# The second network's first loads join a fixed instruction order, and w_v's rebuilding stands behind it

## The chip, the cores and the metric

The kernel runs on one core of a Trainium2 chip. The metric is the device time of one execution in microseconds. A core has a matrix engine (PE), a vector engine (DVE), a scalar engine (ACT), a general engine (POOL) and an engine that issues transfers (SP). Each takes its own instructions in the order in which they stand, and waits on semaphores for the others.

## What is computed

Causal attention with a decay over 32 heads (4 batches of 8 heads, 576 positions, 64 features), then two feed-forward networks. Cut to what matters:

```
attn = softmax(q k^T / 8 + cum_i - cum_j, causal);  x = attn @ v          # 4 x 576 x 512
h = relu(x @ w_in); u, v = split(h)                                       # network 1
x = (u * (w_spatial @ layernorm(v) + b_spatial)) @ w_out
xk = mu_k * x + (1 - mu_k) * x_prev;  xr = mu_r * x + (1 - mu_r) * x_prev # network 2
out = sigmoid(xr @ w_r) * (relu(xk @ w_k)^2 @ w_v)
```

The weights come as 64-bit numbers.

## The kernel before, in words

*Work and names.* Attention goes by pairs of heads. `s` and `t` are scores and transposed scores (matmuls of `kT`, `qT` and the helper rows `kA`, `qA`), `nm` and `mrow` their row maxima, which go through a DRAM buffer `md` into `qA`, and `e` the exponentials; pv multiplies `e` by `v` into `o`. Between them PE does network 1 for the batches that are ready: m1v and m1u are the two halves of x @ w_in (`xt` by `win`), evacuated by ACT into `v` and `u`; `mv` is the normalization of `v`, `vn` its result; m2 (`m<-wspT,vn` in the profile) multiplies by w_spatial, and DVE multiplies its result into `u` (`u<-m,sw,u`). The products go to DRAM as `gd`.

*The second part.* It goes by five chunks of 512 positions. m3(i) loads a chunk as four `g` from `gd`, and splits each into a high and a low part (`gh`): ACT casts, DVE subtracts. It then multiplies by w_out in 48 matmuls. `mix` makes `xx`; m4, m5 and m6 multiply by w_k, w_v and w_r. A weight is rebuilt in blocks of 128x512 by `weights2`: a load into one of two staging buffers `wst`, one ACT and three DVE instructions into `we`, and a split by ACT and DVE into the weight (`moe_w_v` and so on in the profile). Some blocks are rebuilt early, during attention (`emoe_w_k`).

*What sets the order.* Every operation up to the end of network 1 is recorded (class `Planned`) and issued by a list of numbers, `ORDER`, written out by hand; each is held in that place on its engine (`keep_in_program_order`). What comes after `k.nc.issue()` is traced directly, and a scheduler may place it between or ahead of the fixed ones. In the kernel before, m3(0) and w_v's rebuilding are such free work. w_k's and w_r's rebuilding is recorded. `SLOTS` says which buffer each recorded tile takes. The helper through which recorded and pinned operations are issued has line 291, direct ones have line 305 (292 and 306 after the change).

Of the kernel before, what the change touches and what calls it, by code (L numbers as in the profile page):

```python
# [212 lines left out]
]  # L213

# [933 lines left out]
def body(tc, a, out):  # L1148
    k = K(tc, a, out)
# [26 lines left out]
    last = G + 1.45  # L1176
# [20 lines left out]
    for _ in k.m3(0):  # L1197
        next(w2, 0)
# [61 lines left out]
```

## Time and profile before

| | us |
|---|---|
| median of 3 runs (lowest, highest) | 704.87 (704.25, 706.37) |
| the profiled execution | 705.93 |
| its span in the trace | 703.9 |
| PE busy in it | 649.9 (92%) |
| DVE, ACT, POOL busy | 418.8, 373.0, 136.9 |

The span is the time from the first to the last instruction; a little lies around it. All further times are counted from the span's start. PE's work comes to 92% of the span, so what matters is where PE stands idle and what it then waits for. From about 412 us on PE does only the second part.

### The profile page before, as it was taken

The page shows a single profiled execution, that of the slowest core. Times are in us where ns is not written, and L with a number is a line of the kernel's source. Part 1 is how long each engine was busy: PE and PEld are TensorE (multiplying, and loading weights), DVE is VectorE, ACT ScalarE, POOL GpSimd, SP SyncE. Part 2 cuts the span into 40 slices and gives each one's busy share as a digit, 9 for nine tenths or more (in the row PEclk, how much of TensorE's full clock was granted, in tenths as well). Part 3 has the DMA queues.
Part 4 walks back from the last instruction along what each step waited for, and adds up shares of the span by engine and source line. Part 5 has one row for each costly group of instructions (what it writes and reads, how often), then busy time and mean ns, then how long its engine had stood idle before and what let it go on. Part 6 is the DMA issues. An engine that isn't in the chain of part 4 may idle for free.

```text
span 703.9 us, 11693 instructions
## 1 busy us (share of the span) xinstructions
PE 649.9 (92%) x4238; PEld 463.2 (66%) x4238; DVE 418.8 (59%) x1077; ACT 373.0 (53%) x765; POOL 136.9 (19%) x343
## 2 busy tenths in 40 slices
PE   0588899999999899999998699999999999999997
PEld 0245454575655566556756587888888888888896
DVE  7788875896676766770278699355137225522341
ACT  5567875985457653565266387263246225422521
POOL 7012354254234223353322000000000000000000
PEclk9999999999999999999999899999999999999999
DMA  6976766744568437220263742201010100100010
GB/s 210 240 189 175 195 164 172 211 113 103 137 135 214 108 94 147 77 80 22 82 191 98 216 128 82 60 1 61 0 46 10 51 1 15 61 1 0 1 61 30
DMA packets 73615, 70.06 MB, mean 100 GB/s; under 512 B 50883, under 2 KB 51555, under 8 KB 73558
## 3 DMA queue, kind: packets, MB, share of 16 engines
q1 hardware_dynamic: 73126, 68.14, 36.5%
q10 hardware_dynamic: 432, 1.18, 0.5%
q8 instruction: 33, 0.54, 0.3%
q14 instruction: 24, 0.20, 0.1%
HBM read 43.78 MB, written 9.79 MB: 76 GB/s over the span
## 4 chain that ended last, share of the span: by engine, by line
PE 64%; DVE 11%; DMA 10%; ACT 5%; POOL 3%; issue 3%; SPq 3%; POOLq 0%; DVEq 0%; ACTq 0%
PE m L305 43%; PE o L291 5%; PE t L291 4%; PE s L291 3%; PE m1u L291 3%; PE m L291 3%; SPq L291 3%; DMA qA<-md 2%; PE m1v L291 2%; DVE nm L291 1%; DMA v<-in_v_dram 1%; POOL mv L291 1%; DVE junk L291 1%; ACT junka L291 1%; DMA g<-gd 1%
## 5 line engine op out<-in xcount | busy, mean ns | idle before, releaser
L305 PE MATMUL m<-xx,moe_w_k 128*128 128x512 f32 (+1 forms) x480 | 105.5, 369 | 0.0
L305 PE MATMUL m<-moe_w_v,k 128*128 128x512 f32 x432 | 104.3, 390 | 0.0
L305 PEld LDWEIGHTS m<-xx,moe_w_k 128*128 128x128 f32 x480 | 83.9, 188 | 16.2 <-ACT tmp L305 0.2
L305 PEld LDWEIGHTS m<-moe_w_v,k 128*128 128x128 f32 x432 | 80.7, 188 | 17.1
L291 ACT ACTIVATE e<-t,qa 128x512 f32<-128x512 f32 (+1 forms) x128 | 71.4, 591 | 26.8 <-PE t L291 24.0
L305 DVE TENSOR_TENSOR tmp<-tmp 128x512 f32<-128x512 f32 (+1 forms) x40 | 25.4, 638 | 92.9 <-ACT tmp L305 92.7
L291 POOL TENSOR_SCALAR_AFFINE_SELECT e<-e 128x128 f32<-128x128 f32 (+1 forms) x160 | 50.5, 330 | 130.6 <-ACT e L291 129.9
L291 PE MATMUL s<-kT,qT 128*128 128x192 f16 (+3 forms) x192 | 54.2, 291 | 13.6 <-DMA qT<-nq 7.0
L291 DVE CUSTOM_DVE_ANT_0 junk<-s,mask 128x320 bf16<-128x320 f32 (+4 forms) x100 | 47.5, 475 | 29.4 <-PE s L291 27.0
L305 ACT ACTIVATE tmp<-m 128x512 f32<-128x512 f32 (+1 forms) x40 | 22.3, 557 | 78.7 <-PE m L305 77.9
L305 PE MATMUL m<-gh,moe_w_out 128*128 128x512 f32 (+1 forms) x240 | 57.0, 386 | 5.5 <-DVE u L291 5.5
L291 PE MATMUL m1v<-win,xt 128*128 128x512 f16 x240 | 56.7, 379 | 0.0
L291 PE MATMUL m<-wspT,vn 128*128 128x288 f16 x384 | 54.2, 286 | 1.3 <-ACT u L291 1.1
L291 PE MATMUL m1u<-xt,win 128*128 128x288 f16 x384 | 52.8, 286 | 2.4 <-ACT u L291 2.3
L291 PE MATMUL t<-qA,kA 69*128 69x512 f16 (+2 forms) x192 | 48.6, 285 | 6.8 <-DMA qA<-md 5.2
L305 PEld LDWEIGHTS m<-gh,moe_w_out 128*128 128x128 f32 x240 | 44.1, 196 | 15.6 <-DVE u L291 5.8
L291 PE MATMUL s<-kA,qA 67*128 67x192 f16 (+3 forms) x192 | 49.5, 292 | 3.2 <-DMA qA<-qT 3.2
L291 PE MATMUL o<-e,v 128*64 128x64 f32 (+4 forms) x384 | 51.5, 404 | 0.3 <-ACT sm L291 0.3
L305 PE MATMUL m<-moe_w_r,xx 128*128 128x512 f32 x216 | 51.2, 394 | 0.0
L291 PE MATMUL t<-qT,kT 128*128 128x512 f16 (+2 forms) x192 | 50.1, 285 | 0.0
L305 PEld LDWEIGHTS m<-moe_w_r,xx 128*128 128x128 f32 x216 | 40.4, 187 | 9.9
L291 PEld LDWEIGHTS <-win 128*128 128x128 f16 x384 | 36.2, 98 | 13.4 <-issue 3.1
(162 smaller groups left out, 1065.1 us busy)
## 6 DMA issues: line engine op xcount, KB each, us to landing
knat<-in_k_dram SPq DMA_DIRECT2D x16, 320.0 KB
v<-in_v_dram SPq DMA_DIRECT2D x20, 256.0 KB
sr<-rd SPq DMA_DIRECT2D x32, 144.0 KB
gd<-u SPq DMA_DIRECT2D x16, 288.0 KB
out_dram<-o SPq DMA_DIRECT2D x18, 256.0 KB
qnat<-in_q_dram SPq DMA_DIRECT2D x14, 320.0 KB
wst<-in_moe_w_k_dram SPq DMA_DIRECT2D x8, 512.0 KB
g<-gd SPq DMA_DIRECT2D x16, 256.0 KB
```

The costliest lines, as they stand in the source:

```text
L291: self.tc.keep_in_program_order(fn(*map(now, a), **{x: now(y) for x, y in kw.items()}))
L305: return fn(*map(now, a), **{x: now(y) for x, y in kw.items()})
```

## The change

Three things are done. The first part of m3(0), its four loads, four casts and four subtracts, is recorded as a step `gh0` and has places in `ORDER`; the matmuls follow as before. The ACT instruction and the first DVE instruction that rebuild a block of w_v are pinned behind all that was issued before them. And `ORDER` has new numbers throughout, from the start of attention to the end of network 1 (4221 entries instead of 4209). Of the list one line is shown.

```diff
 ORDER = [
     0, 2, 9, 8, 10, 11, 1, 12, 4, 13, 14, 3, 6, 5, 7, 17, 15, 16, 29, 18, 30, 19, 20, 40,
...
-    57, 56, 36, 99, 47, 52, 54, 53, 71, 100, 101, 37, 55, 61, 72, 73, 62, 38, 233, 74, 102, 59, 103, 245,
...
+    57, 56, 71, 99, 47, 52, 54, 53, 100, 101, 36, 72, 73, 59, 55, 61, 37, 233, 102, 103, 245, 253, 74, 62,
...
     ('wstage2', 'wst'): [0, 1, 0, 1, 0, 1, 0, 1],
+    ('phase3', 'g'): [0, 1, 0, 1],
     ('wstage2', 'we'): [0, 1, 0, 1, 0, 1, 0],
...
+    def gh0(self):
+        self.m30 = self.m3(0)
+        next(self.m30)
+
...
     w2 = k.weights2(wp, ("moe_w_out", "moe2_w_k", "moe2_w_r"), wst, True)
     next(w2)
+    k.add(last + 2.6, 9, k.gh0)
     last += 1.65
...
-    w2b = k.weights2(k.p2, ("moe2_w_v",), wst)
+    w2b = k.weights2(k.p2, ("moe2_w_v",), wst, True)
     wrest = (x for w in (w2, w2b) for x in w)
-    for _ in k.m3(0):
+    for _ in k.m30:
         next(w2, 0)
```

DVE at the end of network 1, before: L305 rows are the free work, here w_v's; `u<-m_...,sw,u` is the evacuation of m2.

```order
L291 SCALAR_TENSOR_TENSOR u<-m_5014,sw,u 128x288
L291 TENSOR_TENSOR moe_w_r<-we,moe_w_r 128x512
L291 SCALAR_TENSOR_TENSOR u<-m_5032,sw,u 128x288
L305 TENSOR_SCALAR wst<-wst 128x512
L291 SCALAR_TENSOR_TENSOR u<-m_5050,sw,u 128x288
L291 TENSOR_SCALAR wst<-wst 128x512
L305 SCALAR_TENSOR_TENSOR we<-we,wst 128x512
```

The same place after the change:

```order
L292 SCALAR_TENSOR_TENSOR u<-m_5030,sw,u 128x288
L292 TENSOR_TENSOR moe_w_r<-we,moe_w_r 128x512
L292 SCALAR_TENSOR_TENSOR u<-m_5048,sw,u 128x288
L292 SCALAR_TENSOR_TENSOR u<-m_5067,sw,u 128x288
L292 TENSOR_SCALAR wst<-wst 128x512
L292 SCALAR_TENSOR_TENSOR we<-we,wst 128x512
L292 SCALAR_TENSOR_TENSOR we<-wst,we 128x512
L292 TENSOR_TENSOR moe_w_r<-we,moe_w_r 128x512
L306 SCALAR_TENSOR_TENSOR tmp<-x_5115,mu,tmp 128x511
L306 TENSOR_TENSOR xx_5162<-tmp,xx_5162 128x512
```

The first instruction on w_v stood ahead of the last `u`; after the change the last two `u` are neighbours, then come w_r's last block and the mixing, and w_v's first instruction stands 22 rows behind the last `u`.

ACT where m1v's results are evacuated, before: `gh<-g` are the casts of m3(0)'s loads.

```order
L291 CAST moe_w_k<-emoe_w_k_3799 128x512
L291 ACTIVATE v_4628<-m1v,ds 128x512
L291 CAST moe_w_k<-emoe_w_k_4008 128x512
L291 CAST moe_w_k<-emoe_w_k_4140 128x512
L305 CAST gh<-g 128x512 x2
L291 ACTIVATE v_4628<-m1v,ds 128x512
L291 ACTIVATE mv<-mv,eps 128x1
L291 ACTIVATE we<-wst 128x512
L291 ACTIVATE mv<-mv 128x1
```

The same place after the change:

```order
L292 CAST moe_w_k<-emoe_w_k_4117 128x512
L292 ACTIVATE v_4634<-m1v,ds 128x512
L292 ACTIVATE we<-wst 128x512
L292 ACTIVATE mv<-mv,eps 128x1
L292 ACTIVATE mv<-mv 128x1
L292 ACTIVATE v_4634<-m1v,ds 128x512
L292 ACTIVATE we<-wst 128x512
L292 CAST gh<-g 128x512
L292 ACTIVATE v_4634<-m1v,ds 128x512
L292 CAST vn<-v_4634 128x512
L292 ACTIVATE mv<-mv,eps 128x1
L292 CAST gh<-g 128x512
```

The two casts stood together ahead of the second `v`; now the second `v`, two `we` and two `mv` are ahead of the first cast, and the casts stand singly.

PE in the middle of attention, before, where `t` waits at 220.60 us (`m1v` is network 1, `o<-e,v` is pv):

```order
L291 LDWEIGHTS xt_209
L291 MATMUL m1v<-win,xt_209 128x512
L291 LDWEIGHTS kA_162
L291 MATMUL t<-qA_260,kA_162 128x512
L291 LDWEIGHTS kT_157
L291 MATMUL t<-qT_285,kT_157 128x512
```

The same place after the change:

```order
L292 LDWEIGHTS xt_209
L292 MATMUL m1v<-win,xt_209 128x512
L292 MATMUL o<-e,v_258 64x320 x2
L292 MATMUL o<-e,v_258 64x192 x2
L292 MATMUL o<-e,v_258 64x64 x2
L292 LDWEIGHTS kA_162
L292 MATMUL t<-qA_265,kA_162 128x512
L292 LDWEIGHTS kT_157
L292 MATMUL t<-qT_292,kT_157 128x512
```

Six matmuls of pv stand ahead of the first `t`, which had stood behind it.

## Rows read from the trace of the kernel before

**Rows 1.** The page's first line.

```profile
span 703.9 us, 11693 instructions
```

**Rows 2.** Stages: PE, PEld, DVE, ACT, POOL busy (instructions), granted clock, DMA share, GB/s.

```profile
250.00:350.00 100.00, 99.43 (x864) 64.37 (x863) 53.04 (x175) 47.40 (x102) 35.10 (x82) 1.00 0.35 88
350.00:412.00 62.00, 53.00 (x321) 37.31 (x319) 47.08 (x90) 35.08 (x70) 9.68 (x26) 0.94 0.50 151
412.00:704.00 292.00, 288.04 (x1322) 237.39 (x1320) 130.40 (x237) 119.21 (x218) 1.03 (x4) 1.00 0.10 35
```

**Rows 3.** PE's waits from 350 to 412 us: total, times, longest.

```profile
PE m L305 <- DVE u L291: 5.5, 1, 5.5
PE m1u L291 <- ACT u L291: 2.3, 1, 2.3
PE m L291 <- ACT u L291: 1.1, 1, 1.1
```

**Rows 4.** PE's timeline: start, duration, instruction, idle time before.

```profile
371.68 6.04 PE L291 MATMUL m1u<-xt,win 128*128 128x288 f16 x48 [2.33 <-ACT u L291]
378.86 1.63 PE L291 MATMUL m<-wspT,vn 128*128 128x288 f16 x12 [1.14 <-ACT u L291]
...
398.27 14.07 PE L305 MATMUL m<-gh,moe_w_out 128*128 128x512 f32 x48 [5.53 <-DVE u L291]
```

**Rows 5.** ACT's timeline from 350 us.

```profile
359.96 1.27 ACT L305 CAST gh<-g 128x512 fp32r<-128x512 f32 x2 [4.43 <-DMA g<-gd]
361.13 0.68 ACT L291 ACTIVATE v<-m1v,ds 128x512 f32<-128x512 f32 x1
...
361.90 0.65 ACT L291 ACTIVATE we<-wst 128x512 f32<-128x512 f32 x1
...
371.14 0.49 ACT L291 ACTIVATE u<-m1u,ds 128x288 f32<-128x288 f32 x1
```

**Rows 6.** DVE's timeline at the end of network 1.

```profile
394.15 0.51 DVE L291 SCALAR_TENSOR_TENSOR u<-m,sw,u 128x288 f32<-128x288 f32 x1
397.36 0.43 DVE L305 TENSOR_SCALAR wst<-wst 128x512 int32<-128x512 int32 x1 [2.70 <-DMA wst<-in_moe_w_v_dram]
397.70 0.51 DVE L291 SCALAR_TENSOR_TENSOR u<-m,sw,u 128x288 f32<-128x288 f32 x1
398.13 0.42 DVE L291 TENSOR_SCALAR wst<-wst 128x512 int32<-128x512 int32 x1
```

**Rows 7.** The chain that ended last, 374 to 400 us: start, duration, piece.

```profile
392.95 4.38 DMA wst<-in_moe_w_v_dram
```

**Rows 8.** Short windows, columns as in rows 2: the clock after waits.

```profile
398.20:404.00 5.80, 5.73 (x14) 4.48 (x15) 4.04 (x8) 1.35 (x3) 0.00 (x0) 0.50 0.58 194
...
412.00:424.00 12.00, 12.00 (x53) 9.51 (x52) 11.80 (x22) 10.26 (x19) 0.45 (x1) 1.00 0.57 178
369.00:372.00 3.00, 0.67 (x6) 0.41 (x5) 3.00 (x8) 2.14 (x6) 2.21 (x7) 1.00 0.21 72
...
110.50:113.90 3.40, 3.40 (x31) 1.69 (x30) 2.23 (x11) 0.64 (x3) 0.00 (x0) 0.50 0.60 134
```

**Rows 9.** PE's timeline in the first chunk of the second part.

```profile
431.83 2.02 PE L305 MATMUL m<-moe_w_v,k 128*128 128x512 f32 x8
...
445.68 2.91 PE L305 MATMUL m<-xx,moe_w_k 128*128 128x512 f32 x12
448.43 2.90 PE L305 MATMUL m<-moe_w_v,k 128*128 128x512 f32 x12
```

**Rows 10.** PE's waits from 40 to 350 us.

```profile
PE t L291 <- DMA qA<-md: 5.2, 5, 1.4
```

**Rows 11.** PE's timeline in attention.

```profile
110.17 0.30 PE L291 MATMUL s<-kT,qT 128*128 128x320 f16 x1 [1.63 <-DVE nm L291]
...
220.60 0.38 PE L291 MATMUL t<-qA,kA 69*128 69x512 f16 x1 [1.03 <-DMA qA<-md]
```

**Rows 12.** Waits up to 45 us.

```profile
PE s L291 <- DMA qA<-qT: 3.2, 1, 3.2
```

264 rows, old and new, of tables (ORDER, SLOTS) are left out of this document.

## The prediction

> **What bounds the kernel now.** I read the stages first. From 412 us on PE is busy in 288 of 292 us, from 250 to 350 us in 99.43 of 100; from 350 to 412 us it is busy in only 53.0 of 62 [rows 2]. So the end is set by PE's work plus PE's idle time, and the largest idle stretch after the start-up is the passage from the attention to the first weights of the second part. The list of PE's waits there has three entries, 2.3, 1.1 and 5.5 us: twice for ACT's `u`, once for DVE's `u` [rows 3]. The timeline places them: ahead of the second 48 m1u matmuls at 371.68, ahead of m2 at 378.86, and 5.53 us ahead of m3(0) at 398.27 [rows 4]. Each delays all that PE does afterwards, since PE does not wait again to speak of.
>
> Then I looked at what ACT and DVE were doing. ACT stood idle for 4.43 us and cast the first two `gh` at 359.96, when their load landed; the second `v` had to come behind them, at 361.13, and the first `u` at 371.14 [rows 5]. DVE had all but one `u` of network 1 done at 394.15; then an instruction of w_v's rebuilding, at 397.36, waited 2.70 us for its load, and the last `u` came behind it at 397.70 [rows 6]. That load was issued at 392.95 and took 4.38 us [rows 7]: three of the 5.53 us are a transfer that m3(0) has no use for.
>
> Last the clock. From 398.20 to 404 us the granted clock was 0.50, the lower of its two levels (1.2 GHz); from 412 to 424 it was 1.00, the higher (2.4 GHz) [rows 8]. The 48 matmuls of m3(0) took 14.07 us [rows 4]; at full clock 53 such matmuls take 12.00 us [rows 8], 0.226 each, and 48 take 10.9. So 3.2 us more were lost behind the gap.
>
> **The change part by part.** *(1) `gh`'s casts take places in the order.* On ACT they now stand behind two `v`, two `we` and two `mv`, and singly. A `v` with an `mv` behind it takes 361.90 - 361.13 = 0.77 us, a `we` some 0.56 (its 0.65 less the 0.1 by which such instructions overlap, as I estimate it) [rows 5]; 2 x 0.77 + 2 x 0.56 = 2.7 us. They fill 2.7 of the 4.43 us that ACT stood idle; one `gh` still holds ACT until 359.96. What follows comes 2.7 us earlier, the first `u` too. PE then finds it done at about 368.9, before its first 48 m1u matmuls end at 371.68 - 2.33 = 369.35, and the first wait vanishes. It reaches m2 2.33 us earlier, but the `u` that m2 waits for is 2.7 us earlier, so of the second wait 2.33 + 1.14 - 2.7 = 0.8 us stays, and m2 starts 2.7 us earlier. Term: 2.7 us. Bounds: 0, if another chain, that of the `mv` through DVE and POOL, sets the `u` anyway, and 3.5, both waits gone.
>
> The four loads and four subtracts that are recorded with them are the same ones as before. On SP the first two `g` stand where they stood, behind the two w_k loads; so nothing waits for them that did not before.
>
> *(2) w_v held behind the order.* The last `u` follows the one of 394.15, whose next instruction could start 0.43 us later (by the step from 397.70 to the next row, of the same kind [rows 6]), at 394.6 instead of 397.70: 3.1 us. Behind it DVE now has w_r's last block and the mixing, which m4 needs. Whether everything ahead of that `u` also comes 2.7 us earlier depends on w_r's loads, each of which waits for one of two staging buffers; these are freed by conversions that stand in the same order and come earlier too. I take the whole 2.7, so m3(0) starts 2.7 + 3.1 = 5.8 us earlier, at 392.5; the lower bound is 3.1, w_r's loads where they were.
>
> What w_v's delay costs: nothing, because PE has other work. The first m5 matmul runs at 431.83 [rows 9], and after the change at about 423. In the new order 34 DVE instructions, taken at the 0.65 us of a 128x512 `we` [rows 5], follow the last `u` up to the end of w_v's first block: 34 x 0.65 = 22 us after 392, at 414. That cover of 9 us, less what DVE waits in between, is the estimate on which the worst rival below turns.
>
> *(3) The clock.* The gap before m3(0) shrinks from 5.53 to 5.53 - 3.1 = 2.4 us. The gap of 2.33 us that ends at 371.68 left the clock at 1.00 [rows 4, 8]; against it stands 0.50 from 110.5 to 113.9 us behind a wait of 1.63 [rows 8, 11]. The gap of 2.33 is the nearer row: it followed a long run of matmuls, as the new one will. So I take full clock: 3.2 us. Bound: 0.
>
> The Trainium skill, page "TensorE: Matmul & The Clock Gate", section "Part 1: The HAM clock gate", says that idling puts the array back to half rate, that sustained activity releases it, and that the window it is watched in runs freely, so that the moment varies. The trace agrees on two levels, 1.00 and 0.50 [rows 8]. By that rule a gap of 2.4 us may or may not be punished, depending on where it falls: the sum would be 11.0 or 7.8 us. It is the first rival.
>
> *(4) The order laid out anew in attention.* PE's `t` matmuls waited for DMA qA<-md five times from 40 to 350 us, 5.2 us in all [rows 10], 1.03 of it at 220.60 [rows 11]. At three of the five places the new order puts other matmuls ahead of the waiting `t` (at 220.60 six of pv, at the two others m1u). At about 1.0 us each (5.2 / 5) that is worth up to 3; since what is put there is taken from a later place, I take half, 1.5. At the start the first `s<-kA` waited 3.2 us for qA<-qT [rows 12]; `nq` is now finished three DVE instructions earlier and its transfers go ahead of cumd. That is worth between 0 and 3.2; I take 0.5, since many other waits follow that one. Bounds for the whole: +6 (3 and 3.2) and -4: were the 100 us from 250, in which PE was idle for 0.57 [rows 2], stripped of the work that filled them, they could take on waits like the five, at most some four of 1.0.
>
> **Sum.** 2.7 + 3.1 + 3.2 + 2.0 = 11.0 us. The profiled execution took 705.93 us, 2.0 more than its span of 703.9 [rows 1]; it would take 694.9, with a span of 692.9. It was 1.06 us above the median of the runs, 704.87; from that the forecast is 693.9 us.
>
> **The rivals.** *The clock falls all the same:* all else as above, 3.2 us less: 697.1 us. For it speaks the stretch at 110 us.
>
> *w_r's loads set the last `u`:* m2 ends earlier but the last `u` stays at 394.6; then the gap is 5.53 + 2.7 - 3.1 = 5.1 us, the clock falls, and the gain is 3.1 + 2.0 = 5.1: 699.8 us. For it speaks that w_r's conversions stand between the `u` on DVE in both orders; against it, that their loads wait for conversions which move.
>
> *No change:* w_r's loads set the last `u`, and attention loses its 4 us instead of gaining 2: 3.1 - 4 = -0.9, about 705.8 us, within what can be told from no change.
>
> *Slower: w_v too late.* After w_v is held back, PE reaches an m5 before its weights are rebuilt. m4 and m5 blocks alternate at 448.43 - 445.68 = 2.75 us each [rows 9], so PE wants a block of w_v each 5.5 us. A block is a load of 4.4 us [rows 7], a DVE instruction of 0.43 [rows 6] and five more on DVE and ACT at about 0.65 (the `we` in rows 5). With two buffers these overlap and a block takes about half of their sum, 4 us; one after another they take 4.4 + 0.43 + 5 x 0.65 = 8.1, and eight blocks lose 8 x (8.1 - 5.5) = 21 us, less a cover of 5 to 9 us: 12 to 16 us, against a gain of 11. It would end at 706 to 710 us. With 5 us of cover it decides at 5.5 + (11 + 5) / 8 = 7.5 us a block. Against it: the two staging buffers are there as before, and DVE and ACT, 130 and 119 us busy of 292 [rows 2], have time to spare.
>
> *More:* attention's bound of +6 instead of 2 holds: 4 us more, 689.9, and with the second `u` wait gone too 689.1 us.
>
> **How the numbers follow.** The forecast, with a range of its own from 691 to 696, gets 0.47; the clock rival 0.19, w_r's loads 0.13; more than forecast 0.07; no change 0.07; slower 0.07. A measurement of this kernel can tell about 0.3%, 2.1 us, from no change: 702.8 to 707.0. Faster has 0.47 + 0.19 + 0.13 + 0.07 = 0.86, within 0.07, slower 0.07. The range from 688.5 to 700 leaves out no change, slower and a small part of the others.
>
> **What would show it.** Right: PE's list of waits after the attention without 2.3 and without 5.5 for DVE's `u`; the last two `u` on DVE directly one behind the other, w_v's conversion later; one `gh` alone at about 360 on ACT; granted clock 1.00 under m3(0), and its 48 matmuls in 11 us; no PE wait for moe_w_v. Wrong: m3(0) starting at 395 behind w_r, 0.50 under it, PE waits with moe_w_v in their name after 415 us, or new waits of PE between 250 and 350 us.

## The result and the profile after

The changed kernel took 696.16 us, median of 4 runs (693.02 to 698.28), beside 704.56 (702.93 to 706.37) for the kernel before: ratio 0.9864 [0.9832, 0.9896], 1.4% faster, 8.4 us. Run again in two later sets with the kernel before, it gave 0.9810 and 0.9844; the mean of the three is 0.984, 11.3 us. The forecast was 693.9, the sum 11.0 us. The profiled execution, 697.71 us, is one of the slower of its four. The page's first line after, for [rows 1]:

```profile
span 696.0 us, 11688 instructions
```

PE's list of waits after the change, from 330 to 412 us (total, times, longest), has one entry where [rows 3] had three:

```profile
PE m L306 <- DVE u L292: 2.1, 1, 2.1
```

Of its timeline (start, duration, instruction, idle time before) these rows answer to [rows 4, 9]:

```profile
351.10 13.11 PE L292 MATMUL m1v<-win,xt 128*128 128x512 f16 x60
364.05 11.92 PE L292 MATMUL m1u<-xt,win 128*128 128x288 f16 x96
375.81 1.63 PE L292 MATMUL m<-wspT,vn 128*128 128x288 f16 x12
...
391.79 13.01 PE L306 MATMUL m<-gh,moe_w_out 128*128 128x512 f32 x48 [2.10 <-DVE u L292]
404.64 4.29 PE L306 MATMUL m<-xx,moe_w_k 128*128 128x512 f32 x18
...
425.37 1.09 PE L306 MATMUL m<-moe_w_v,k 128*128 128x512 f32 x4
```

All 96 m1u run on without a wait, m2 follows at once, and m3(0) waits 2.10 us instead of 5.53. The last m1v matmuls before the passage began at 350.36 before, 0.74 us earlier than here. So attention itself came no sooner in this pair, and everything gained in it lies behind: from there to m3(0) it is 40.69 us instead of 47.91, to m4 53.54 instead of 61.82.

ACT's timeline after, for [rows 5]:

```profile
357.60 0.67 ACT L292 ACTIVATE v<-m1v,ds 128x512 f32<-128x512 f32 x1
358.64 0.70 ACT L292 ACTIVATE we<-wst 128x512 f32<-128x512 f32 x1 [0.37 <-DMA wst<-in_moe_w_k_dram]
359.29 0.62 ACT L292 CAST gh<-g 128x512 fp32r<-128x512 f32 x1
...
367.14 0.89 ACT L292 ACTIVATE u<-m1u,ds 128x288 f32<-128x288 f32 x2
```

The second `v` comes at 357.60 instead of 361.13, the first `u` at 367.14 instead of 371.14; the 4.43 us of idle time ahead of the cast are gone, and the cast no longer waits at all. Of ACT's time, 1.64 and 0.37 us now go to waits for the two w_k loads ahead of `we`. DVE's timeline after, for [rows 6], with w_v's first block:

```profile
389.43 0.51 DVE L292 SCALAR_TENSOR_TENSOR u<-m,sw,u 128x288 f32<-128x288 f32 x1
390.19 0.69 DVE L292 TENSOR_TENSOR moe_w_r<-we,moe_w_r 128x512 fp32r<-128x512 f32 x1 [0.25 <-ACT moe_w_r L292]
390.81 0.93 DVE L292 SCALAR_TENSOR_TENSOR u<-m,sw,u 128x288 f32<-128x288 f32 x2
...
416.31 0.42 DVE L306 TENSOR_SCALAR wst<-wst 128x512 int32<-128x512 int32 x1
...
420.89 0.68 DVE L306 TENSOR_TENSOR moe_w_v<-we,moe_w_v 128x512 fp32r<-128x512 f32 x1
```

The last two `u` stand together, and the first block of w_v is done at 420.89 + 0.68 = 421.6, 3.8 us before PE's first m5 at 425.37.

Windows of the trace after, columns as in [rows 2]; the second and third answer to the first of [rows 8], the last two to those of [rows 2]:

```profile
75.00:80.00 5.00, 3.92 (x30) 1.87 (x27) 4.24 (x12) 5.00 (x12) 3.82 (x8) 1.00 1.13 299
391.80:396.00 4.20, 4.20 (x11) 3.30 (x12) 2.35 (x4) 0.62 (x1) 0.00 (x0) 0.59 0.90 285
396.00:404.60 8.60, 8.60 (x38) 6.96 (x37) 3.64 (x5) 5.54 (x9) 0.00 (x0) 1.00 0.10 38
250.00:350.00 100.00, 97.58 (x847) 62.97 (x846) 54.22 (x175) 49.35 (x103) 36.76 (x85) 1.00 0.32 79
350.00:412.00 62.00, 59.90 (x360) 43.30 (x358) 48.83 (x92) 40.81 (x78) 8.86 (x27) 0.97 0.51 149
```

The clock still fell behind the gap: 0.59 granted over the first 4.2 us of m3(0), 1.00 after that. PE is now idle for 2.1 us from 350 to 412 (it was 9.0), but for 2.42 from 250 to 350 (it was 0.57).

### The profile page after: what moved, and what is told of

Read it like the earlier page. It is cut to its first block, busy times and chain, and to the rows that moved or that the text cites. A ratio compares the mean times of both kernels' runs of the same rounds, so it can differ in the third digit from the quotient of the medians.

```text
span 696.0 us, 11688 instructions
## 1 busy us (share of the span) xinstructions
PE 646.5 (93%) x4238; PEld 462.4 (66%) x4238; DVE 419.4 (60%) x1077; ACT 375.8 (54%) x765; POOL 138.7 (20%) x343
## 4 chain that ended last, share of the span: by engine, by line
PE 65%; DVE 12%; DMA 10%; ACT 5%; POOL 3%; SPq 3%; issue 3%; DVEq 0%; POOLq 0%; ACTq 0%
PE m L306 43%; PE o L292 6%; PE t L292 4%; PE s L292 4%; PE m1u L292 3%; DMA wst<-in_moe_w_k_dram 3%; DMA qA<-md 3%; SPq L292 3%; PE m L292 3%; DVE nm L292 2%; POOL mv L292 2%; DMA knat<-in_k_dram 1%; PE m1v L292 1%; DMA sr<-rd 1%; DVE junk L292 1%
## 5 line engine op out<-in xcount | busy, mean ns | idle before, releaser
L292 POOL TENSOR_SCALAR_AFFINE_SELECT e<-e 128x128 f32<-128x128 f32 (+1 forms) x160 | 53.2, 347 | 133.2 <-ACT e L292 132.3
L292 PE MATMUL s<-kT,qT 128*128 128x64 f16 (+3 forms) x192 | 54.4, 293 | 12.5 <-DVE nm L292 7.2
L292 DVE CUSTOM_DVE_ANT_0 junk<-s,mask 128x512 bf16<-128x512 f32 (+4 forms) x100 | 47.5, 475 | 23.4 <-PE s L292 20.4
L306 PE MATMUL m<-gh,moe_w_out 128*128 128x512 f32 (+1 forms) x240 | 55.5, 381 | 2.1 <-DVE u L292 2.1
L292 PE MATMUL s<-kA,qA 67*128 67x64 f16 (+4 forms) x192 | 49.8, 293 | 1.4 <-DMA kA<-cumd 1.4
L292 PEld LDWEIGHTS o<-e,v 128*64 128x64 f32 x384 | 24.7, 136 | 29.8 <-issue 18.6
```

Source lines behind the costliest of these rows:

```text
L292: self.tc.keep_in_program_order(fn(*map(now, a), **{x: now(y) for x, y in kw.items()}))
L306: return fn(*map(now, a), **{x: now(y) for x, y in kw.items()})
```

## The experiments

Every ratio is to the kernel before, run on the same chip beside it (its median was 704.78 to 708.26 us in the later sets, so a ratio does not follow from the 704.56 of the first row). In all kernels the whole reference is computed. Where the passage is spoken of, it is counted from the start of the last m1v.

| kernel | median us | ratio [95%] | m1v to m3(0) | gap | m3(0) | m1v to m4 |
|---|---|---|---|---|---|---|
| before | 704.56 | | 47.91 | 5.53 | 14.07 | 61.82 |
| after | 696.16 | 0.9864 [0.9832, 0.9896] | 40.69 | 2.10 | 13.01 | 53.54 |
| after_again | 692.29 | 0.9810 [0.9783, 0.9837] | 39.54 | 0.94 | 11.47 | 50.84 |
| after_third | 694.50 | 0.9844 [0.9811, 0.9878] | 39.79 | 1.20 | 11.47 | 51.09 |
| pin_only | 702.25 | 0.9940 [0.9914, 0.9966] | 43.61 | 2.53 | 13.00 | 56.44 |
| no_pin | 701.62 | 0.9939 [0.9918, 0.9961] | 44.20 | 5.61 | 13.55 | 57.59 |
| old_order_pin | 703.31 | 0.9963 [0.9942, 0.9985] | 47.21 | 2.65 | 13.00 | 60.05 |
| old_order_nopin | 707.35 | 1.0019 [0.9995, 1.0042] | 46.50 | 2.56 | 13.01 | 59.35 |
| gh_first | 699.17 | 0.9900 [0.9878, 0.9922] | 43.64 | 2.66 | 13.02 | 56.50 |
| old_attention | 698.34 | 0.9894 [0.9867, 0.9920] | 41.20 | 2.57 | 13.01 | 54.04 |
| old_attention_again | 698.39 | 0.9874 [0.9831, 0.9916] | 40.40 | 1.80 | 11.46 | 51.70 |
| freebank | 693.12 | 0.9819 [0.9798, 0.9839] | 38.34 | none | 11.51 | 49.68 |
| freebank_again | 692.39 | 0.9822 [0.9790, 0.9855] | 38.34 | none | 11.46 | 49.64 |
| pin_bank | 699.49 | 0.9915 [0.9885, 0.9946] | 42.29 | none | 11.55 (47 of the 48) | 53.68 |

**pin_only: the kernel before with w_v held back, nothing else.**

```diff
-    w2b = k.weights2(k.p2, ("moe2_w_v",), wst)
+    w2b = k.weights2(k.p2, ("moe2_w_v",), wst, True)
```

> The kernel before with w_v's rebuilding pinned and nothing else. My theory: the two waits of PE for ACT's u (2.3 and 1.1 us) stay, the last u of DVE follows its neighbour, m3(0) starts 3.1 us earlier (395.2 us), the gap is 2.4 us, the clock still falls for part of m3(0), about 13.0 us instead of 14.07: 4.2 us faster than before. Rival (w_r's loads set the last u): the gap stays near 5 us and the gain is under 1 us.

0.9940, 4.2 us. The gap is 2.53 instead of 5.53, while the two waits for ACT's `u` stay. PE's waits from 350 us:

```profile
PE m L305 <- DVE u L291: 2.5, 1, 2.5
PE m L291 <- ACT u L291: 1.1, 1, 1.1
PE m1u L291 <- ACT u L291: 1.0, 1, 1.0
```

The second term stands by itself, without the new order, at 3.0 us of gap and 1.1 under m3(0). The first wait for ACT's `u` is 1.04 here instead of 2.33, which the pin does not explain: the load of the first `g` ended ACT's wait 8.01 us behind the last m1v (364.43) instead of 9.60, and m2 starts 27.20 us behind it instead of 28.50. So the old order itself varies by over 1 us up to m2.

**no_pin: the changed kernel with the True of that line taken out again.**

> The changed kernel without the pin on w_v. w_v's first two DVE instructions then stand ahead of the last u again. Theory: that u waits for w_v's load, which is issued at about 390 and takes 4.4 us; m3(0) starts near 396 instead of 391.8, behind a gap over 6 us, at half clock for longer: 5 us slower than the changed kernel. Rival (the pin only moves work that is hidden): the same time within 1 us.

0.9939. PE's only wait from 350 to 412 us is the one ahead of m3(0), 5.6 us, as long as before the change; DVE's timeline shows why:

```profile
391.09 0.43 DVE L306 TENSOR_SCALAR wst<-wst 128x512 int32<-128x512 int32 x1 [2.81 <-DMA wst<-in_moe_w_v_dram]
...
392.47 0.51 DVE L292 SCALAR_TENSOR_TENSOR u<-m,sw,u 128x288 f32<-128x288 f32 x1
```

Without the pin the free instruction goes ahead of the last `u` again, and DVE waits for its load. The pin is worth (0.9939 - 0.9840) x 705 = 7.0 us in the new order against 4.2 in the old one. From the table against the mean of the three afters: 4.2 of gap, 1.6 under m3(0), and 0.9 behind m4 (292.3 to the end of the span instead of 291.4), 6.7.

**old_order_pin and old_order_nopin: the old list, with `gh`'s twelve operations put into it at places I chose, with and without the pin.**

```diff
-    3875, 3732, 3789, 3934, 3790, 4026, 3729, 3791, 3908, 3952, 3792, 3793, 3794, 3731, 3981, 3935, 3795, 3796, 3803, 3797, 3953, 3798, 3799, 3996,
+    3875, 3732, 3789, 3934, 3790, 4038, 3946, 3949, 3729, 3791, 3908, 3964, 3792, 3793, 3794, 3731, 3993, 3935, 3795, 3796, 3803, 3797, 3965, 3798,
...
+    k.add(last + 2.6, 9, k.gh0)
...
-    for _ in k.m3(0):
+    for _ in k.m30:
```

> The order of before for all that it had, gh's twelve operations put in at the places that they have in the changed order, and the pin: the change without the order laid out anew. Theory from the two traces: attention's new order brings nothing (PE reaches the last m1v 0.7 us later than before), so this kernel is within 1 us of the changed one, or up to 1 us faster; the waits for ACT's u are gone or under 1 us. Rival (my prediction's fourth term): the new order is worth 2 us, and this kernel is 2 us slower than the changed one.

> As the one before it, without the pin; here the scheduler happens to put w_v's first instruction behind the last u on its own. Theory: it is the place that counts, not the pin, so the last u is not held up and the time is that of the pinned one within 1 us. Rival: w_v's blocks among the mixing delay m4 or help it, over 1 us either way.

Both missed their times, though in the second the rival came true: it was 4 us slower than the pinned one. The casts do not stand where the changed order has them, although the expectation says that they do. PE waited longer for the first `u` than before: `PE m1u <- ACT u` is 3.9 us in the first. ACT's timeline in old_order_pin:

```profile
361.17 0.62 ACT L292 CAST gh<-g 128x512 fp32r<-128x512 f32 x1 [1.96 <-DMA g<-gd]
...
367.27 0.62 ACT L292 CAST gh<-g 128x512 fp32r<-128x512 f32 x1 [3.21 <-DMA g<-gd]
...
372.43 0.62 ACT L292 CAST gh<-g 128x512 fp32r<-128x512 f32 x1 [1.91 <-DMA g<-gd]
...
373.79 0.49 ACT L292 ACTIVATE u<-m1u,ds 128x288 f32<-128x288 f32 x1
```

My places for the third and fourth cast were ahead of their loads, and ACT stood 3.21 and 1.91 us in them with the `u` behind. So these two say nothing on the change's own places, but they do say that a fixed place alone is not what helps: it must be one at which the load has landed. In old_order_nopin the gap was 2.56 without the pin. There w_v's first instructions went in among the mixing, and from m4 on it took 294.2 us instead of 291.4; why the scheduler chose so is open.

**gh_first: the changed kernel with the first two casts back in one piece behind the first `v`.**

The two casts, 3947 and 3950, are taken from their later places further down the list.

```diff
-    3785, 3964, 3786, 3949, 3729, 3787, 3731, 3908, 3788, 3993, 3779, 3789, 3790, 3935, 4008, 3791, 3792, 3793, 4023, 3965, 3794, 3795, 3803, 3796,
+    3785, 3964, 3786, 3949, 3729, 3787, 3731, 3908, 3788, 3993, 3779, 3789, 3790, 3935, 4008, 3791, 3792, 3793, 4023, 3965, 3794, 3795, 3803, 3947,
+    3950, 3796, 3994, 3797, 3798, 4039, 3816, 3799, 3800, 3801, 4009, 3802, 3804, 3805, 3817, 4024, 3806, 3818, 3807, 3819, 3808, 3820, 4040, 3825,
...
```

> The changed kernel with the first two casts of gh moved on ACT to where they were before, ahead of the second v; all else in the changed order. Theory (my first term): ACT stands still again until g lands, v and with it u come later, a wait of PE for ACT's u between 1 and 3 us comes back, and the stretch from m1v to m3(0) is 2 to 3 us longer than 40.7. Rival: the u are held by other things that the new order mended, and the stretch stays within 0.7 us of 40.7.

0.9900: of 11.3 us 7.0 are left. The first line is ACT's, and PE's timeline has the waits back that the change had removed:

```profile
359.07 0.62 ACT L292 CAST gh<-g 128x512 fp32r<-128x512 f32 x1 [4.09 <-DMA g<-gd]
```

```profile
370.97 6.04 PE L292 MATMUL m1u<-xt,win 128*128 128x288 f16 x48 [0.48 <-ACT u L292]
377.97 1.63 PE L292 MATMUL m<-wspT,vn 128*128 128x288 f16 x12 [0.95 <-ACT u L292]
```

From the last m1v to m2 it takes 377.97 - 351.50 = 26.47 us: 1.8 more than after (24.71), and 2.0 less than before (378.86 - 350.36 = 28.50). So two casts in the wrong place give back about half of what was gained up to m2. Where the other half comes from is not shown: the load of `g` also ended ACT's wait sooner here, 7.57 us behind the last m1v instead of 9.60, and in the old order m2 comes sooner by as much when that load does (8.01 us and 27.20 in pin_only, 9.59 and 28.67 in pin_bank). Up to m3(0) the two casts cost 3.0 to 4.1 us, since the gap there is 2.66 again.

**old_attention and its repeat: the old list up to the end of attention's part (entry 3767), the changed one from there, with `gh` and the pin.**

> The order of before up to its entry 3767, at the end of attention, and the changed order from there on, with gh and the pin. Theory: the gain lies in the tail, from the last m1v to m3(0), which takes 40.7 us after the change and 47.9 before; so this kernel has a tail of 40.7 +- 0.5 and is within 2 us of the changed one. Rival: the order laid out anew in attention is a large part of the gain, and this kernel is 3 to 6 us slower than the changed one.

> The old order up to the end of attention with the changed tail, a second time, since the part of attention in the gain rests on one comparison so far: 0.9894 of before against 0.9864, 0.9810 and 0.9844 for the changed kernel, mean 0.984. Theory: the order laid out anew in attention is worth 2 to 6 us, so the ratio is 0.987 to 0.992. Rival (attention is worth nothing, the last comparison was chance): 0.984.

0.9894 and 0.9874, mean 0.9884, beside 0.9840 for the three of the changed kernel: the new order of attention is worth 0.0044 x 705 = 3.1 us, by the intervals anything from about 1 to 5. The first of the two expectations missed its time, and its rival, 3 to 6 us slower, came true. The passage was nearly as short as with the whole change (54.04 and 51.70). I could not find the 3 us in one place: see the fourth term below.

**freebank: the changed kernel, with a PSUM bank for m3(0)'s first group that no `u` has to leave first.** In both kernels the PSUM pool of the second part is opened where those of the first were closed. Here `pso`, the pool of pv's results, long idle by then, is opened ahead of the others and kept open, and m3(0)'s first group is written into it. m5's first two accumulators are put into it as well. (A bank is the piece of PSUM, the memory into which PE writes its results, that one group of matmuls fills.)

```diff
...
-            ps = self.ps3.tile([128, 512], F32, tag="p", bufs=4, name="m3")
+            if i == 0 and m == 0:
+                ps = self.pso.tile([128, 1024], F32, tag="o", bufs=1, name="m3")
+            else:
+                ps = self.ps3.tile([128, 512], F32, tag="p", bufs=4, name="m3")
...
+                if fc == 0 and j == 0:
+                    o2 = self.pso.tile([128, 1024], F32, tag="o", bufs=1, name="m5")
                 if fc == 0:
-                    acc.append(self.ps3.tile([128, 512], F32, tag=f"a{j}", bufs=1, name=f"m5_{j}"))
+                    acc.append(o2[:, 512 * j:512 * j + 512] if j < 2 else self.ps3.tile([128, 512], F32, tag=f"a{j}", bufs=1, name=f"m5_{j}"))
...
-    for p in (k.pso, k.pst, k.pss, k.psm, k.es, k.acts, k.w):
+    for p in (k.pst, k.pss, k.psm, k.es, k.acts, k.w):
...
-    for p in (k.ps3, k.p2, wst, k.p3, wp, k.hl, k.c):
+    for p in (k.ps3, k.pso, k.p2, wst, k.p3, wp, k.hl, k.c):
```

> The changed kernel, with the first of m3(0)'s four groups in a PSUM bank that attention's o had, so that it need not wait for the last u to leave its bank. Theory: m3(0) has no use for the last u's data and waits for its bank alone; it follows m2 with no gap, the clock stays at 1.00, m3(0) takes 10.9 us instead of 13.0, and the kernel is 2.1 + 2.1 = 4.2 us faster than the changed one. Rival: the mixing or m4's weights (w_r's last block on DVE) then become the bound, and PE waits for them behind m3(0): a gain under 1.5 us.

> The changed kernel with the first group of m3(0) in the bank of attention's o, once more beside the changed kernel. Theory: the gap and the half clock behind it are gone in every execution, so it is 1 to 3 us faster than the changed kernel on average, with a smaller spread (0.5 us in four executions before, against 6). Rival: the same time within 1 us, since the gap was short in most executions of the changed kernel.

0.9819 and 0.9822. PE's timeline and then DVE's, in freebank:

```profile
387.16 0.41 PE L292 MATMUL m<-wspT,v 128*128 128x288 f16 x2
387.31 11.51 PE L306 MATMUL m<-gh,moe_w_out 128*128 128x512 f32 x48
398.65 1.54 PE L306 MATMUL m<-xx,moe_w_k 128*128 128x512 f32 x6
```

```profile
388.54 0.69 DVE L292 TENSOR_TENSOR moe_w_r<-we,moe_w_r 128x512 fp32r<-128x512 f32 x1 [0.26 <-ACT moe_w_r L292]
389.15 0.94 DVE L292 SCALAR_TENSOR_TENSOR u<-m,sw,u 128x288 f32<-128x288 f32 x2
```

m3(0) begins right behind m2, 1.8 us before DVE begins the last two `u`. So m3(0) never needed that `u` as data: it waited for the bank that the `u` reads. The gap is gone, and the 48 matmuls run in 11.5 us. Some of it is given back: from m4 to the end it takes 292.2 to 292.6 us instead of 291.4; the cause is open, and m5's accumulators in the shared tile are a candidate that no run tests. The ratios lie within those of the changed kernel (0.9810 to 0.9864), so as a gain beyond the change it is not told apart: the 4.2 us of the first expectation did not come, and the small spread of the first four executions (692.9 to 693.4) was not repeated (691.4 to 695.5).

**pin_bank: pin_only with the same edit.**

> The kernel before with the pin on w_v and the first group of m3(0) in the PSUM bank of attention's o; its order is the old one. Theory: m3(0) waits only for a bank, in the old order too; it follows m2 with no gap at full clock, 11.5 us, so from the last m1v to the first m4 it takes 42.4 + 11.5 = 53.9 us against 61.8 before and 56.4 with the pin alone: 2.5 us faster than the pin alone, 6 to 8 us faster than before. Rival: PE then waits behind the first group for the last u, or m4 for the mixing, and the gain over the pin alone is under 1 us.

0.9915, 6.0 us, 1.8 more than pin_only by the ratios, whose intervals overlap: m1v to m4 in 53.68, against 56.44 in pin_only and 53.54 in the profiled changed kernel. The waits for ACT's `u` stay (1.7 and 1.1 us). One matmul of m3(0) ran ahead already at 369.00, in the first of them. Two small edits and the old order thus make up about half of the change's gain.

**after_again and after_third: the changed kernel unaltered.**

> The changed kernel once more, unaltered, beside the others on one chip: 0.9864 of before by the first measurement. It tells how far executions of one program lie apart in the attention, since two profiled executions of the same attention order reached the last m1v at 350.4 and 356.4 us.

> The changed kernel unaltered, for the comparison with the one before it in this list on the same chip: 0.981 to 0.986 of before, executions spread over some 6 us.

0.9810 and 0.9844; the interval of the first only just touches that of the 0.9864 expected. PE's timelines of these two:

```profile
386.39 11.47 PE L306 MATMUL m<-gh,moe_w_out 128*128 128x512 f32 x48 [0.94 <-DVE u L292]
```

```profile
392.46 11.47 PE L306 MATMUL m<-gh,moe_w_out 128*128 128x512 f32 x48 [1.20 <-DVE u L292]
```

Here the gap is half as long and the clock does not fall. The two begin m3(0) 39.54 and 39.79 us behind the last m1v instead of 40.69. What sets the gap can be read in the chain that ended last, in the first trace of the changed kernel (start, duration, piece):

```profile
351.92 6.69 DMA wst<-in_moe_w_k_dram
...
382.71 4.12 DMA wst<-in_moe_w_r_dram
...
390.89 0.86 DVE u L292 x2
```

A load of w_r lands at 386.83, DVE's instruction on it starts at 386.85, and from there DVE works with 0.25 us of idle time up to the last `u`. In all nine traces with a gap of 0.94 to 2.66 us, m3(0) starts 4.94 or 4.95 us behind that DVE instruction. That instruction starts 11.04 us behind the start of m2 in the first trace of the changed kernel, 9.88 and 10.13 in the other two, and the gaps differ by as much, within 0.01. The chain leads back to a load of w_k: DVE's instruction on that one starts 7.54, 6.34 and 6.52 us behind the last m1v, and 28.2 to 28.4 us lie between the two in the three traces, and in those of no_pin, freebank and freebank_again. In gh_first, where the two casts stand between, they are 31.8 us apart, and the gap is 2.66. No run moves these loads alone.

## Why the prediction was right, and where its sum was not

The time was forecast at 693.9 and measured at 696.16, with repeats at 692.29 and 694.50. The first lies just above the 691 to 696 that the prediction gave the forecast itself, and nearer to the 697.1 of the clock rival, whose half clock the profiled execution shows; the repeats lie inside. The sum by its terms:

| term | predicted | profiled pair | mean of three after |
|---|---|---|---|
| 1: `gh`'s casts (m1v to m2) | 2.7 | 3.8 | 3.8 |
| 2: last `u` (m2 to m3(0)) | 3.1 | 3.4 | 4.1 |
| 3: clock (m3(0) to m4) | 3.2 | 1.1 | 2.1 |
| 4: attention (arrival at the last m1v) | 2.0 | -0.7 | 1.5 (7 traces of each order) |
| from m4 on | 0 | 0.4 | 0.4 |
| sum | 11.0 | 8.0 | 11.9 |

The sum of the profiled pair is the difference of its spans, 703.9 - 696.0 = 7.9; the mean ratio gives 11.3.

*Term 1 held, and was sized low.* Both waits for ACT's `u` went, and m2 starts 24.71 us behind the last m1v in all three traces, 28.50 before (against the 27.20 and 28.67 that the same old order gave in pin_only and pin_bank, the term would be 2.5 and 4.0). The working took 2.7 because one cast was to wait for its load until 359.96; it did not wait (359.29, no idle time). The bound of 3.5 fell 0.3 short. gh_first shows that the places of the casts are worth 1.8 of it up to m2, and 3.0 to 4.1 us up to m3(0).

*Term 2 held.* 3.0 us by pin_only alone, 3.4 here, and no_pin brings the gap back to 5.61. The place in the order and the pin go together: the pin alone gained 4.2 us, all but the pin 4.3, both 11.3 (the 2.8 us above their sum are no larger than what the intervals leave open). The rival that w_r's loads set the last `u` was right in its mechanism and wrong in its size. The load moved with the rest, as the prediction took it to: DVE's instruction on it starts 35.75 us behind the last m1v instead of 39.84. But when it lands sets the gap that remains (see after_again).

*Term 3 is the one that was mis-sized*: 1.1 in the profiled run, 2.1 on average. The failed step is "the gap of 2.33 is the nearer row". A gap like it ahead of m3(0) was punished every time: six traces with gaps of 2.10 to 2.66 give 13.00 to 13.02 us for the 48 matmuls. Gaps of 0.94, 1.20 and 1.80, or none, give 11.46 to 11.55. So the first rival was right on the clock for a gap of the estimated size. That the repeats still came out near the forecast is luck: their gaps were about half of the 2.4 estimated, and terms 1 and 2 were sized low. Full clock was sized wrongly too: 11.5 us, not 10.9, for the 48 matmuls, since the 53 of the window [rows 8] count those that only reach into it.

The Trainium skill, page "TensorE: Matmul & The Clock Gate", section "Part 1: The HAM clock gate", says that the moment at which the clock changes varies, since its window runs freely. That 2.33 us ahead of m1u left the clock at 1.00 [rows 4, 8] would fit it, but does not show it; m3(0) does not bear it out, since six traces agree within 0.02 us there.

*Term 4 is right in sign by the ratios, and its working holds only in part.* In this pair the waits for DMA qA<-md did not go: PE's list from 40 to 350 us after has

```profile
PE t L292 <- DMA qA<-md: 6.1, 5, 2.1
```

as against 5.2 in five [rows 10]. Over seven traces of each order they do shrink, from 6.5 us on average (5.1 to 7.5) to 4.5 (2.9 to 6.1), close to the 1.5 taken. But all of PE's waits in this list come to 14.4 and 14.2 us: others stand in their place. At the start nothing was gained: up to 45 us qA<-qT's 3.2 [rows 12] have gone, yet the whole list comes to 28.0 us after and 27.5 before. Of its entries, before and then after:

```profile
PE tot L291 <- POOL identb L291: 7.1, 1, 7.1
PE tot L291 <- ACT junka L291: 7.0, 3, 3.3
```

```profile
PE tot L292 <- ACT junka L292: 14.2, 3, 7.2
...
PE s L292 <- DVE nm L292: 4.5, 3, 3.1
```

In the 100 us from 250 PE is idle for 1.9 us more, as the prediction's lower bound feared in kind. Against it stands the clock: before, 75 to 80 and 110 to 115 us had 0.66 granted, and after both are at 1.00. Over all traces, the seven with the old order of attention have eight such stretches of 5 us between 70 and 210 us (from 0.66 to 0.74), the seven with the new one two (0.68 and 0.70). At 0.66 a stretch loses some 5 x 0.34 = 1.7 us of PE's work, as I estimate it, so eight less two over seven are 1.5 us: that may be part of the 3. But the arrival at the last m1v varies for one and the same order from 349.33 to 356.42 (old) and from 346.85 to 352.67 (new), with means of 351.8 and 350.3, so these 1.5 us are not told apart from the scatter. The size is thus between 1 and 5 us by the ratios, and the cause stays open.

*The slower rival did not come.* PE has no wait for w_v. But its cover was 3.8 us and not the 9 estimated: DVE did its 34 instructions with waits between them, as the estimate had left out.

## What to carry to other kernels

A free instruction that waits for a load, and that a scheduler may put ahead of fixed work on an in-order engine, costs what is left of that load (2.7 us here): look for the first one behind which the path stands, and pin it. A fixed place helps only where its operand is there by then. And where a matmul waits for an evacuation, ask first whether it needs the data or only the bank: the bank can be had elsewhere.

## What the runs showed of the hardware that was not expected

The cost of a gap ahead of m3(0) does not grow with it from 2.10 to 2.66 us: with 1.80 us of idle time or less the 48 matmuls took 11.5 us, with 2.10 already 13.01, with 2.66 still 13.02; only the gaps of 5.53 and 5.61 cost more, 14.07 and 13.55. Ahead of m1u 2.33 us [rows 4] cost nothing [rows 8], but 3.35 and 3.88 us did, in the two kernels with the old order and placed casts: the 48 matmuls behind took 7.71 us instead of 6.04, with 0.65 and 0.66 granted over the first 3.7. What decides between the two places (what PE did before, or when the gap fell) was not tried.

The same program reaches the last m1v as much as 5.8 us apart in three executions (346.85, 351.10, 352.67), with nothing changed, and takes 291.3 to 291.4 us from m4 on in all of them: most of the scatter of this kernel's time is made in the attention, and up to 2.7 us of it between the last m1v and m4. A change of 1 or 2 us there can't be read from one pair of traces.
